# Gate and value products by Strassen's method in a fused attention and two-MLP kernel

## Chip, cores and metric

One NeuronCore of a Trainium2 chip runs the whole program. The metric is the device time of one execution in microseconds (us); the kernel before takes 590.2 us, the median of 3 runs (589.99 to 590.84).

## What is computed

```python
attn = softmax(mask(q @ k.T / 8)) @ v          # 2 batches, 12 heads, 448 tokens, 64 wide
x = rows of 768 (12 heads x 64) for 896 tokens
h = x @ w_in;  y = (h * clip(h + 3, 0, 6) / 6) @ w_out             # 768 -> 2048 -> 768
xn = y / sqrt(mean(y * y) + 1e-6) * rms_g
out = (silu(xn @ w_gate) * (xn @ w_val)) @ w_out2                  # 768 -> 1536 -> 768
```

The weights come as float64 and are narrowed to float32 on the chip.

## The kernel before

Activations lie transposed: features on the partitions, tokens along the row. The 896 tokens are two groups g of 448 columns, so that one PSUM bank (128 x 448 float32) is one output tile of a group. Each float32 operand is split into a high half (a cast to fp32r) and a low half (the rest), and a product of two tiles is three matmuls (`mm3`, lines 199 to 208): high by high, high weights by low, low weights by high.

The work runs in this order: attention for both groups with the first MLP's first layer of group 0 laid between its steps; `ff1_in(1)` (16 tiles of 18 matmuls); `ff1_out(0)` and `ff1_out(1)` (6 tiles of 48 matmuls each); `ff2_in` (lines 592 to 603: 12 weight columns m, gate and value, both groups, 48 tiles of 18 matmuls); and `strassen` (lines 498 to 522: the last product by Strassen's method in its Winograd form, 7 products of 54 matmuls).

The order on every engine's queue is written by hand. The program counts steps (lines 83 to 97 and 700 to 711); in a step after attention nine matmuls are issued, and `at(delay, fn)` puts other work at the head of a later step, in the order in which it was asked for. An engine takes its instructions strictly in that order. A tile of 18 matmuls is two steps.

Weights pass through `w_load` (line 116, a DMA), `w_split` and `narrowed` (lines 135 to 159: two passes over the 64-bit words, on ScalarE, or one of them on GpSimd where `beside` is set), `w_join` (line 165, VectorE), `w_halves` (line 176, ScalarE cast) and `w_low` (line 183, VectorE subtraction). Three weight tiles are split ahead of their use; there are four buffers for halves (NW), three for raw words (NRAW), three for narrowed tiles (NC_BUF). `w_tile` (line 191) asks for the next split when a tile is first used. `b_prepare` to `b_keep` (lines 211 to 261) narrow the last weight, form Strassen's sums of it and store them in DRAM; this runs every 6 steps from the middle of `ff1_out(1)` into `ff2_in`.

The RMS norm is applied late. `ff1_y` and `ff1_ylow` (lines 558 to 574) multiply y by rms_g, split it and sum the squares on GpSimd; `rms_sum` (a matmul with ones), `rms_root` and `rms_inv` (lines 576 to 587) make the inverse root, and `ff2_gate` and `ff2_val` (lines 605 to 625) multiply it onto each output tile. The left operands of the last product and their sums (`sums_first` to `sums_third`, lines 455 to 475) stay in SBUF until `a_split` and `a_low` (lines 477 to 494) halve them.

Of the kernel before, what the change touches and what calls it, by code (L numbers as in the profile page):

```python
# [9 lines left out]
F32 = mybir.dt.float32  # L10
# [38 lines left out]
def fused_kernel(ctx: ExitStack, tc, qa, qb, ka, kb, v, w_in, w_out, w_gate, w_val, w_out2, rms_g, out):  # L49
# [36 lines left out]
    def at(delay, fn, *args):  # L86
        due[clock["now"] + delay].append((fn, args))
# [18 lines left out]
    for m in range(NF2):  # L106
        srcs += [w_gate[m], w_val[m]]
    srcs += [(p, n) for p in ORDER for n in range(NN)]
    IN2 = 4 * NP1
    OUT2 = IN2 + 2 * NF2  # L110
    raws, plain, splits = {}, {}, {}

    apart = {n: APART for n in range(NW - 1)}
    state = {"load": 0, "split": 0}

    def w_load():
        n = state["load"]
        if n >= len(srcs):
# [12 lines left out]
        c = wpool.tile([128, 768], F32, tag="c", name=f"c{n}", bufs=NC_BUF)  # L131
        nc.sync.dma_start(c, src)
        plain[n] = c

    def w_split():

        n = state["split"]
        if n >= len(srcs):
# [51 lines left out]

    def w_tile(n, j):

        if n not in used:
# [16 lines left out]

    def b_prepare(column, part):

        raw = wpool.tile([128, 768, 2], U32, tag="braw", name=f"braw{column}_{part}", bufs=1)
# [235 lines left out]
        for k in range(NF1):  # L449
            gs.pop((g, k))  # L450

    left, halves = {"split": set()}, {}
    SOURCE = {1: (0, 0), 2: (0, 1), 4: (1, 1), 7: (1, 0)}

    def sums_first(p):

        t = slot([128, NT], f"s1_{p}")
        nc.vector.tensor_add(t, left[1, 2 * p], left[1, 2 * p + 1])
        left["s1", p] = t
        nc.vector.tensor_sub(left[1, 2 * p], left[0, 2 * p], left[1, 2 * p])  # L460
        at(1, sums_second, p)

    def sums_second(p):
        if (1, p) not in left["split"]:
            at(1, sums_second, p)
            return
        a = left[0, 2 * p]
        nc.vector.tensor_sub(a, left["s1", p], a)
        left["s2", p] = a
        at(1, sums_third, p)  # L470

    def sums_third(p):
        t = slot([128, NT], f"s4_{p}")
        nc.vector.tensor_sub(t, left[0, 2 * p + 1], left["s2", p])
        left["s4", p] = t

    def a_split(q, p):

        key = {5: ("s1", p), 6: ("s2", p), 3: ("s4", p)}.get(q)
        if key is None:  # L480
            g, odd = SOURCE[q]
            key = (g, 2 * p + odd)
        src = left[key]
# [4 lines left out]
        at(1, a_low, q, p, key, hi, lo, src)  # L488

    def a_low(q, p, key, hi, lo, src):  # L490
        nc.vector.tensor_sub(lo, src, f32(hi))
        left["split"].add((q, p))
        if q != 1:
            left.pop(key)

    bank, held = {}, {}

    def strassen(w0):

        kps = NF2 // 2  # L500
        seen = set()
        for i, q in enumerate(ORDER):
            if i + 1 < len(ORDER):
                for p in range(kps):
                    at(1 + p, a_split, ORDER[i + 1], p)
            for n in range(NN):
# [49 lines left out]
                ff2_store(0, 2 * n, ps)  # L556

    def ff1_y(g, m, ps):
        hi = slot([128, NT], f"yhi{g}_{m}", F32R)
        nc.scalar.mul(hi, ps, gvec[:, m:m + 1])  # L560
        s = slot([128, NT], f"sq{g}_{m}")
        nc.scalar.activation(s, ps, AF.Square)
        at(1, ff1_ylow, g, m, ps, hi, s)

    def ff1_ylow(g, m, ps, hi, s):
        lo = slot([128, NT], f"ylo{g}_{m}", F32R)
        nc.vector.scalar_tensor_tensor(lo, ps, gvec[:, m:m + 1], f32(hi), ALU.mult, ALU.subtract)
        ys[g, m] = (hi, lo)
        if m == 0:
            ri[g] = s  # L570
            return
        nc.gpsimd.tensor_add(ri[g], ri[g], s)
        if m == NK - 1:
            at(2, rms_sum, g)

    def rms_sum(g):
        ps = psum(f"n{g}")[:, :NT]
# [14 lines left out]
    def ff2_in(w0):
        for m in range(NF2):
            for n in range(2):
                for g in range(2):
                    ps = psum(f"f{g}_{m}_{n}")[:, :NT]
                    ks = range(NK)
                    for k in ks:
                        yield from mm3(ps, w_tile(w0 + 2 * m + n, k), ys[g, k], k == ks[0], k == ks[-1])
                    if n == 0:  # L600
                        at(1, ff2_gate, g, m, ps)
                    else:
                        at(2, ff2_val, g, m, ps)

    def ff2_gate(g, m, ps):
        if g not in inverse:
            at(1, ff2_gate, g, m, ps)
            return
        t = slot([128, NT], f"t{g}_{m}")
        nc.vector.tensor_mul(t, ps, ri[g])  # L610
        ss[g, m] = t
        at(1, ff2_silu, t)

    def ff2_silu(t):
        nc.scalar.activation(t, t, AF.Silu)

    def ff2_val(g, m, ps):
        t = slot([128, NT], f"u{g}_{m}")
        nc.vector.tensor_mul(t, ps, ri[g])
        nc.vector.tensor_mul(t, t, ss.pop((g, m)))  # L620
        left[g, m] = t
        if g == 0 and m % 2 == 0:
            at(1, a_split, 1, m // 2)
        if g == 1 and m % 2 == 1:
            at(2, sums_first, m // 2)

    def ff2_store(g, m, o):
        dst = out[m * 128:(m + 1) * 128, g * NT:(g + 1) * NT]
# [9 lines left out]
        nc.sync.dma_start(dst[:, a], o[:, a])  # L638
        nc.scalar.dma_start(dst[:, b], o[:, b])

    def products():
        yield from ff1_in(0, 0)
        yield from ff1_in(1, NP1)
        yield from ff1_out(0, 2 * NP1)
        for i in range(2 * NK):
            n, rest = divmod(i, 4)
            at(PREP + BETWEEN * i, b_prepare, 2 * n + rest % 2, rest // 2)
        yield from ff1_out(1, 3 * NP1)
        yield from ff2_in(IN2)
        yield from strassen(OUT2)  # L650

    with tc.manual_schedule():
# [115 lines left out]
```

## Time and profile before

| | us |
|---|---|
| median of the runs | 590.2 |
| the profiled execution | 589.9 |
| its span, first to last instruction | 588.1 |
| TensorE (PE) busy in the span | 578.7 |
| VectorE (DVE) busy | 375.2 |
| ScalarE (ACT) busy | 356.5 |
| GpSimd (POOL) busy | 87.2 |

The mean granted TensorE clock is 0.997 of full speed. A busy time is the sum of an engine's instruction times in the span; matmuls are pipelined, so that one lasts about twice the distance to the next, and the pace is read from their starts. A row of a group gives line, engine, operation, output and inputs, shape, count, busy time in us, mean ns of one, and then the engine's idle time before it with what ended it.

### The profile page before, as it was taken

The page shows a single profiled execution, that of the slowest core. Times are in us where ns is not written, and L with a number is a line of the kernel's source. Part 1 is how long each engine was busy: PE and PEld are TensorE (multiplying, and loading weights), DVE is VectorE, ACT ScalarE, POOL GpSimd, SP SyncE. Part 2 cuts the span into 40 slices and gives each one's busy share as a digit, 9 for nine tenths or more (in the row PEclk, how much of TensorE's full clock was granted, in tenths as well). Part 3 has the DMA queues.
Part 4 walks back from the last instruction along what each step waited for, and adds up shares of the span by engine and source line. Part 5 has one row for each costly group of instructions (what it writes and reads, how often), then busy time and mean ns, then how long its engine had stood idle before and what let it go on. Part 6 is the DMA issues. An engine that isn't in the chain of part 4 may idle for free.

```text
span 588.1 us, 8933 instructions
## 1 busy us (share of the span) xinstructions
PE 578.7 (98%) x3138; PEld 507.6 (86%) x3138; DVE 375.2 (64%) x712; ACT 356.5 (61%) x682; POOL 87.2 (15%) x132
## 2 busy tenths in 40 slices
PE   8899999999999999999999999999999999999997
PEld 6557777778899999999999999999999999999996
DVE  4767777676455576664466677978665655675861
ACT  7998888887455587774355885565444432354440
POOL 5665444544000000101010100000000000000000
PEclk9999999999999999999999999999999999999999
DMA  8968776762233469975668966875623202133531
GB/s 229 283 191 253 228 248 205 236 196 86 68 111 116 190 242 319 330 251 169 238 209 321 341 204 229 301 249 175 204 91 126 81 28 81 54 111 106 171 116 64
DMA packets 41149, 109.52 MB, mean 186 GB/s; under 512 B 5648, under 2 KB 20176, under 8 KB 41104
## 3 DMA queue, kind: packets, MB, share of 16 engines
q1 hardware_dynamic: 40672, 108.60, 55.7%
q8 instruction: 25, 0.41, 0.3%
q10 hardware_dynamic: 432, 0.34, 0.2%
q14 instruction: 20, 0.16, 0.1%
HBM read 85.33 MB, written 23.59 MB: 185 GB/s over the span
## 4 chain that ended last, share of the span: by engine, by line
PE 93%; ACT 6%; issue 1%; DVE 0%; DVEq 0%
PE f L203 10%; PE f L207 10%; PE f L205 10%; PE y L203 8%; PE y L207 8%; PE y L205 8%; PE h L207 7%; PE h L203 7%; PE h L205 7%; ACT sm L330 4%; PE o L390 3%; PE t L364 3%; PE s L313 3%; PE z L203 1%; PE z L207 1%; PE z L205 1%
## 5 line engine op out<-in xcount | busy, mean ns | idle before, releaser
L179 ACT CAST whi<-c 128x768 fp32r<-128x768 f32 x109 | 90.9, 834 | 94.0 <-DVE c L163 50.5
L185 DVE TENSOR_TENSOR wlo<-c,whi 128x768 fp32r<-128x768 f32 x109 | 108.3, 994 | 27.5 <-ACT whi L179 24.0
L203 PE MATMUL f<-yhi,whi 128*128 128x448 f32 x288 | 105.8, 367 | 0.0
L207 PE MATMUL f<-yhi,wlo 128*128 128x448 f32 x288 | 104.9, 364 | 0.0
L205 PE MATMUL f<-ylo,whi 128*128 128x448 f32 x288 | 104.0, 361 | 0.0
L207 PE MATMUL h<-xh,wlo 128*128 128x448 f32 x192 | 72.0, 375 | 0.0
L205 PE MATMUL h<-xl,whi 128*128 128x448 f32 x192 | 70.9, 369 | 0.0
L203 PE MATMUL y<-ghi,whi 128*128 128x448 f32 x192 | 70.5, 367 | 0.0
L203 PE MATMUL h<-xh,whi 128*128 128x448 f32 x192 | 70.4, 367 | 0.0
L207 PE MATMUL y<-ghi,wlo 128*128 128x448 f32 x192 | 70.0, 365 | 0.0
L205 PE MATMUL y<-glo,whi 128*128 128x448 f32 x192 | 69.3, 361 | 0.0
L163 DVE SCALAR_TENSOR_TENSOR c<-c,raw 128x768 uint32<-128x768 uint32 x56 | 55.7, 995 | 19.0 <-ACT raw L158 12.7
L348 POOL TENSOR_SCALAR sm<-sm,st 112x112 f32<-112x112 f32 (+1 forms) x96 | 55.9, 601 | 68.2 <-ACT pt L374 28.8
L207 PEld LDWEIGHTS f<-yhi,wlo 128*128 128x128 f32 x288 | 53.9, 187 | 5.4 <-issue 0.2
L205 PEld LDWEIGHTS f<-ylo,whi 128*128 128x128 f32 x288 | 54.1, 188 | 4.0
L203 PEld LDWEIGHTS f<-yhi,whi 128*128 128x128 f32 x288 | 54.1, 188 | 3.7 <-issue 0.2
L154 ACT ACTIVATE c<-raw 128x768 f32<-128x768 f32 x56 | 50.8, 907 | 3.4 <-DVE wlo L185 3.4
L330 ACT ACTIVATE sm<-sm,st 112x112 f32<-112x112 f32 (+3 forms) x96 | 49.6, 525 | 3.5 <-DVE st L323 3.4
L427 DVE SCALAR_TENSOR_TENSOR t<-t,h 128x448 f32<-128x448 f32 x32 | 19.8, 620 | 38.7 <-ACT t L423 38.7
L207 PEld LDWEIGHTS h<-xh,wlo 128*128 128x128 f32 x192 | 36.0, 188 | 9.3 <-issue 6.7
L423 ACT ACTIVATE t<-h,half 128x448 f32<-128x448 f32 x32 | 20.4, 638 | 35.4 <-PE h L207 35.4
L323 DVE CUSTOM_DVE_ANT_0 sm<-s,mask 112x112 f32<-112x112 f32 (+3 forms) x96 | 37.3, 443 | 5.9 <-PE s L313 5.6
(106 smaller groups left out, 954.6 us busy)
## 6 DMA issues: line engine op xcount, KB each, us to landing
raw<-in_w_in SPq DMA_DIRECT2D x16, 768.0 KB, 5.7
raw<-in_w_out SPq DMA_DIRECT2D x16, 768.0 KB, 6.0
braw<-in_w_out SPq DMA_DIRECT2D x12, 768.0 KB, 5.7
raw<-in_w_gate SPq DMA_DIRECT2D x12, 768.0 KB, 5.4
raw<-in_w_val SPq DMA_DIRECT2D x12, 768.0 KB, 5.1
c<-kept SPq DMA_DIRECT2D x21, 384.0 KB, 3.0
keptin<-c SPq DMA_DIRECT2D x16, 384.0 KB, 2.7
c<-keptin SPq DMA_DIRECT2D x16, 384.0 KB, 3.0
```

What stands on the lines that cost most here:

```text
L154: nc.scalar.activation(c, f32(high), AF.Prelu, scale=2.0 ** -112, alpha=2.0 ** 32)
L163: nc.vector.scalar_tensor_tensor(bits, bits, 3, z, ALU.logical_shift_left, ALU.bitwise_or)
L179: nc.scalar.copy(hi, c)
L185: nc.vector.tensor_sub(lo, c, f32(hi))
L203: nc.tensor.matmul(ps, whi, xhi, start=first, stop=False, skip_group_check=again)
L205: nc.tensor.matmul(ps, whi, xlo, start=False, stop=False, skip_group_check=again)
L207: nc.tensor.matmul(ps, wlo, xhi, start=False, stop=last, skip_group_check=again)
L323: nc.vector.tensor_tensor_reduce(dst, src, mask[:, S - n:], scale=-0.125, scalar=3e38, op0=ALU.add, op1=ALU.min, accum_out=st[u][:, 0, c:c ...
L330: nc.scalar.activation(dst, dst, AF.Exp, scale=-1.0, bias=st[u][:, 0, c:c + 1], accum_out=st[u][:, 1, c:c + 1])
L348: nc.gpsimd.tensor_scalar(t[:, o:o + n], t[:, o:o + n], c, 1.0, op0=ALU.mult, op1=ALU.mult)
L423: nc.scalar.activation(t, ps, AF.Relu, bias=half, scale=1.0 / 6.0)
L427: nc.vector.scalar_tensor_tensor(t, t, 1.0, ps, ALU.min, ALU.mult)
```

## The change

Nine of the twelve column pairs (gate m, value m) are no longer 4 tiles of 18 matmuls but 7 Strassen products of 9: the halves of the 768 inputs, gate and value, and the two token groups are the 2 x 2 x 2 blocks. Three pairs stay as they were, ahead of the others and in another order (`ff2_plain`). Three of the seven results are added up in PSUM: ScalarE copies a finished bank into another bank (product 1), or to SBUF before more is added onto the same bank (products 7 and 6). y is multiplied by the inverse root before the layer; its halves and the four sums of its blocks are made there. The weight sums of a pair are made on the chip a block ahead (`pair_begin`), with one narrowing pass on GpSimd. Left operands of the last product go to DRAM and come back, except for the last of six. `b_prepare` is moved ahead: six parts into `ff1_in(1)`, six into `ff1_out(1)`, using the buffers of the raw words. The diff is cut; lines of "..." stand for what is left out: the bodies of the `pair_*` helpers, each one subtraction of 128 x 384 (DVE) or one cast (ACT) and its low half (DVE), and changes of names.

```diff
-PREP, BETWEEN = 4, 6
+PREPS = (2, 4, 6), (1, 3.7, 6)
+PLAIN = 3
...
+    def left_keep(q, p, t):
+        if p == NF2 // 2 - 1:
+            fetched[q, p] = t
+            return
+        d = dram.tile([128, NT], F32, name=f"left{q}_{p}")
+        nc.sync.dma_start(d, t)
+        stored[q, p] = d
...
+    def sums_second(p):
+        a = left.pop((0, 2 * p))
+        nc.vector.tensor_sub(a, left.pop(("s1", p)), a)
+        left_keep(6, p, a)
+        t = slot([128, NT], f"s4_{p}")
+        nc.vector.tensor_sub(t, left.pop((0, 2 * p + 1)), a)
+        left_keep(3, p, t)
...
@@ in strassen(w0) @@
                 for p in range(kps):
                     at(1 + p, a_split, ORDER[i + 1], p)
+                    if p >= 3:
+                        at(p - 2, a_fetch, ORDER[i + 1], p)
+            if i + 2 < len(ORDER):
+                for p in range(3):
+                    at(4 + p, a_fetch, ORDER[i + 2], p)
...
@@ in ff1_y(g, m, ps) @@
+        y = slot([128, NT], f"y{g}_{m}")
+        nc.scalar.mul(y, ps, gvec[:, m:m + 1])
         s = slot([128, NT], f"sq{g}_{m}")
         nc.scalar.activation(s, ps, AF.Square)
+        ys[g, m] = y
...
+        elif m < NK - 1:
+            at(1, rms_add, g, s)
+        else:
+            nc.vector.tensor_add(ri[g], ri[g], s)
+            at(1, rms_sum, g)
...
@@ in rms_root(g, ps) @@
         nc.vector.reciprocal(ri[g], ri[g])
+        for i, k in enumerate((0, 1, 2, 3, 4, 5)):
+            at(1 + (i // 2 if g else 2 * i), y_scale, g, k)
+        if g:
+            for j in range(KH):
+                at(6 + j, y_sums, j)
+    def y_scale(g, k):
+        y = ys[g, k]
+        nc.vector.tensor_mul(y, y, ri[g])
+        at(1, y_split, {(0, 0): 1, (0, 1): 2, (1, 0): 0, (1, 1): 4}[g, k // KH], k % KH, y)
+    def y_split(q, j, src):
...
+        nc.scalar.copy(hi, src)
+        at(1, y_low, q, j, hi, lo, src)
...
+        nc.vector.tensor_sub(lo, src, f32(hi))
+    def y_sums(j):
+        a21, a22 = ys[1, j], ys[1, j + KH]
+        nc.vector.tensor_add(a22, a21, a22)
+        nc.vector.tensor_sub(a21, ys[0, j], a21)
+        at(1, y_split, 5, j, ys[1, j + KH])
+        at(1, y_split, 7, j, ys.pop((1, j)))
+        at(1, y_more, j)
+    def y_more(j):
+        a11, a12 = ys.pop((0, j)), ys.pop((0, j + KH))
+        nc.vector.tensor_sub(a11, ys.pop((1, j + KH)), a11)
+        nc.vector.tensor_sub(a12, a12, a11)
+        at(1, y_split, 6, j, a11)
+        at(2, y_split, 3, j, a12)
+    def ff2_plain(w0):
+        order = [(g, i) for g in range(2) for i in range(4)]
+        order += [(g, i) for i in range(4, 2 * PLAIN) for g in range(2)]
+        for t, (g, i) in enumerate(order):
+            m, n = divmod(i, 2)
...
+            if t == 0:
+                at(1, w_split)
+            elif t in (5, 6) or t >= 8 and t % 2 == 0:
+                splits.pop(w0 + (t - 5 if t < 8 else i - 1), None)
+                at(1, w_split)
...
+    def pair_begin(m):
+        at(1, pair_narrow, m, 0)
+        at(2, pair_narrow, m, 1)
+        at(3, pair_high, m, 0)
+        at(4, pair_first, m)
+        at(5, pair_second, m)
+        at(6, pair_third, m)
+        at(7, pair_high, m, 1)
+        at(8, pair_low, m, 1)
+        if m + 1 < NF2:
+            at(4, pair_load, m + 1, 0)
+            at(5, pair_load, m + 1, 1)
...
+    def ff2_strassen():
+        order = []
+        for m in range(PLAIN, NF2):
+            order.append((1, m))
+            if m > PLAIN:
+                order.append((3, m - 1))
+            order += [(q, m) for q in (7, 6, 2, 5, 4)]
+        order.append((3, NF2 - 1))
...
+            name = {1: "x", 2: "x", 7: "r", 4: "r"}.get(q, "y")
...
+            for j in range(KH):
+                yield from mm3(ps, pair_tile(q, m, j), ops[q, j], q in (1, 7) and j == 0, j == KH - 1,
+                               q not in (1, 7))
...
+            at(1, ff2_combine, q, m)
+    def ff2_combine(q, m):
+        if q == 1:
+            y = spare.pop(0)
+            fb["y", m] = y
+            nc.scalar.copy(y, fb["x", m])
+        elif q == 7:
...
+            nc.scalar.copy(fh["c22", m], fb["r", m])
+        elif q == 6:
...
+            nc.scalar.copy(fh["c21", m], fb["y", m])
+        elif q == 2:
...
+            nc.scalar.activation(fh["s", m], fb.pop(("x", m)), AF.Silu)
+        elif q == 5:
+            t = fh["c22", m]
+            nc.vector.tensor_add(t, fb["y", m], t)
+        elif q == 4:
+            t = fh["c21", m]
+            nc.vector.tensor_add(t, fb.pop(("r", m)), t)
+            at(1, ff2_silu, t)
+            at(2, ff2_out, m)
+        else:
...
+            nc.vector.tensor_mul(t, y, t)
+            spare.append(y)
+            left_ready(0, m, t)
```

## Rows read from the trace of the kernel before

**Rows 1.** The page, busy time (share of the span) and instructions of engines.
```profile
PE 578.7 (98%) x3138; PEld 507.6 (86%) x3138; DVE 375.2 (64%) x712; ACT 356.5 (61%) x682; POOL 87.2 (15%) x132
```
**Rows 2.** The page, chain that ended last: share of the span by engine.
```profile
PE 93%; ACT 6%; issue 1%; DVE 0%; DVEq 0%
```
**Rows 3.** Busy time by stage: `ff1_in(1)`, `ff2_in`, `strassen` (the header names the columns).
```profile
core 0: us, PE busy (x) PEld busy (x) DVE busy (x) ACT busy (x) POOL busy (x), PEclk, DMA share, GB/s
158.00:215.30 57.30, 57.30 (x285) 53.12 (x284) 34.58 (x49) 33.39 (x52) 0.00 (x0) 1.00 0.42 146
...
332.50:508.10 175.60, 175.60 (x869) 162.46 (x868) 116.18 (x174) 88.30 (x119) 1.17 (x1) 1.00 0.48 162
508.10:588.10 80.00, 76.59 (x379) 70.66 (x377) 49.82 (x78) 32.58 (x56) 0.00 (x0) 1.00 0.34 109
```
**Rows 4.** Tiles f and w: duration ns min/median/max, first and last start us.
```profile
L203 PE MATMUL f<-yhi,whi x288: 367/367/368, 332.6 to 507.5; 128*128 128x448 f32 x144
...
L203 PE MATMUL w<-ahi,whi x12: 367/367/368, 508.1 to 514.8; 128*128 128x448 f32 x12
```
**Rows 5.** Timeline of PE around the matmul with ones: start, duration.
```profile
280.50 0.36 PE L205 MATMUL y<-glo,whi 128*128 128x448 f32 x1
280.70 0.91 PE L578 MATMUL n<-sq,ones 128*128 128x448 f32 x2
...
281.65 0.37 PE L203 MATMUL y<-ghi,whi 128*128 128x448 f32 x1
```
**Rows 6.** Groups of DVE instructions, shapes apart.
```profile
L185 DVE TENSOR_TENSOR wlo<-c,whi 128x768 fp32r<-128x768 f32 x109 | 108.3, 994 | 27.5 <-ACT whi L179 24.0 <-PE y L207 1.0
...
L229 DVE SCALAR_TENSOR_TENSOR b<-braw 128x384 uint32<-128x384 uint32 x24 | 12.3, 554 | 6.6 <-ACT braw L158 6.6
...
L474 DVE TENSOR_TENSOR s<-u,u 128x448 f32<-128x448 f32 x6 | 3.7, 616 | 0.0
```
**Rows 7.** Timeline of DVE in `ff2_in`: start, duration.
```profile
342.76 2.95 DVE L586 RECIPROCAL sq<-sq 128x448 f32<-128x448 f32 x1 [0.92 <-ACT sq L582]
345.85 0.62 DVE L610 TENSOR_TENSOR t<-f,sq 128x448 f32<-128x448 f32 x1
...
352.04 0.62 DVE L620 TENSOR_TENSOR u<-u,t 128x448 f32<-128x448 f32 x1
352.58 0.62 DVE L491 TENSOR_TENSOR alo<-u,ahi 128x448 fp32r<-128x448 f32 x1
353.12 0.95 DVE L163 SCALAR_TENSOR_TENSOR c<-c,raw 128x768 uint32<-128x768 uint32 x1
353.99 0.62 DVE L610 TENSOR_TENSOR t<-f,sq 128x448 f32<-128x448 f32 x1
354.52 1.02 DVE L229 SCALAR_TENSOR_TENSOR b<-braw 128x384 uint32<-128x384 uint32 x2
355.45 0.95 DVE L185 TENSOR_TENSOR wlo<-c,whi 128x768 fp32r<-128x768 f32 x1
```
**Rows 8.** Groups of ACT instructions, shapes apart.
```profile
L179 ACT CAST whi<-c 128x768 fp32r<-128x768 f32 x109 | 90.9, 834 | 94.0 <-DVE c L163 50.5 <-PE y L205 22.8 <-PE z L205 9.3
...
L154 ACT ACTIVATE c<-raw 128x768 f32<-128x768 f32 x56 | 50.8, 907 | 3.4 <-DVE wlo L185 3.4
...
L486 ACT CAST ahi<-u 128x448 fp32r<-128x448 f32 x30 | 15.8, 564 | 8.3 <-DVE u L620 8.3
...
L528 ACT COPY e<-w 128x448 f32<-128x448 f32 x2 | 1.1, 534 | 3.9 <-PE w L207 3.9
```
**Rows 9.** Timelines of POOL and DVE where a narrowing on POOL meets a join.
```profile
68.79 0.92 POOL L156 TENSOR_SCALAR raw<-raw 128x768 uint32<-128x768 uint8 x1
...
68.99 1.53 DVE L163 SCALAR_TENSOR_TENSOR c<-c,raw 128x768 uint32<-128x768 uint32 x1 [0.23 <-ACT c L154]
```
**Rows 10.** DMA issues: KB each, median us from issue to landing.
```profile
raw<-in_w_gate SPq DMA_DIRECT2D x12, 768.0 KB, 5.4
...
c<-kept SPq DMA_DIRECT2D x21, 384.0 KB, 3.0
```

More of the change, by code (lines that the diff above doesn't have):

```diff
@@ L105, in fused_kernel @@
         srcs += [a[n] for n in range(NP1)] + [(name, n) for n in range(NP1)]
-    for m in range(NF2):
+    for m in range(PLAIN):
         srcs += [w_gate[m], w_val[m]]
+    IN2 = 4 * NP1
+    OUT2 = IN2 + 2 * PLAIN
     srcs += [(p, n) for p in ORDER for n in range(NN)]
-    IN2 = 4 * NP1
-    OUT2 = IN2 + 2 * NF2
     raws, plain, splits = {}, {}, {}
     apart = {n: APART for n in range(NW - 1)}
-    state = {"load": 0, "split": 0}
+    state = {"load": 0, "split": 0, "limit": OUT2}
     def w_load():
         n = state["load"]
-        if n >= len(srcs):
+        if n >= state["limit"]:
             return
@@ L191, in w_tile @@
     def w_tile(n, j):
-        if n not in used:
+        if n not in used and not IN2 <= n < OUT2:
             used.add(n)
@@ L211, in b_prepare @@
     def b_prepare(column, part):
-        raw = wpool.tile([128, 768, 2], U32, tag="braw", name=f"braw{column}_{part}", bufs=1)
+        raw = wpool.tile([128, 768, 2], U32, tag="raw", name=f"braw{column}_{part}", bufs=NRAW)
         nc.sync.dma_start(raw.rearrange("p n t -> p (n t)"), w_out2[2 * column + part].bitcast(U32))
@@ L450, in ff1_out, with left_ready, a_fetch @@
             gs.pop((g, k))
-    left, halves = {"split": set()}, {}
-    SOURCE = {1: (0, 0), 2: (0, 1), 4: (1, 1), 7: (1, 0)}
+    left, stored, fetched, halves = {}, {}, {}, {}
+    def left_keep(q, p, t):
[5 more added lines that the diff above has]
+        stored[q, p] = d
+    def left_ready(g, m, t):
+        left[g, m] = t
+        p, odd = divmod(m, 2)
+        q = {(0, 0): 1, (0, 1): 2, (1, 1): 4}.get((g, odd))
+        if q:
+            left_keep(q, p, t)
+        if all((i, 2 * p + j) in left for i in range(2) for j in range(2)):
+            at(1, sums_first, p)
     def sums_first(p):
         t = slot([128, NT], f"s1_{p}")
-        nc.vector.tensor_add(t, left[1, 2 * p], left[1, 2 * p + 1])
+        nc.vector.tensor_add(t, left[1, 2 * p], left.pop((1, 2 * p + 1)))
         left["s1", p] = t
-        nc.vector.tensor_sub(left[1, 2 * p], left[0, 2 * p], left[1, 2 * p])
+        left_keep(5, p, t)
+        d = left.pop((1, 2 * p))
+        nc.vector.tensor_sub(d, left[0, 2 * p], d)
+        left_keep(7, p, d)
         at(1, sums_second, p)
     def sums_second(p):
-        if (1, p) not in left["split"]:
-            at(1, sums_second, p)
-            return
[L467 to L475, printed above, removed]
-    def a_split(q, p):
[L479 to L483, printed above, removed]
+        a = left.pop((0, 2 * p))
[4 more added lines that the diff above has]
+        left_keep(3, p, t)
+    def a_fetch(q, p):
+        if p == NF2 // 2 - 1:
+            return
+        t = slot([128, NT], f"a{q}_{p}")
+        nc.sync.dma_start(t, stored.pop((q, p)))
+        fetched[q, p] = t
+    def a_split(q, p):
+        src = fetched.pop((q, p))
         hi = slot([128, NT], f"ahi{q}_{p}", F32R)
@@ new lines, in fused_kernel, with y_low @@
+    done = set()
+    def y_low(q, j, hi, lo, src):
+        nc.vector.tensor_sub(lo, src, f32(hi))
+        done.add((q, j))
+    def y_sums(j):
+        assert (0, j) in done and (4, j) in done
+        a21, a22 = ys[1, j], ys[1, j + KH]
[10 more added lines that the diff above has]
+        at(2, y_split, 3, j, a12)
@@ new lines, in fused_kernel @@
+    ss, spare = {}, []
+    def ff2_plain(w0):
[3 more added lines that the diff above has]
+            m, n = divmod(i, 2)
+            if t < 2:
+                splits.pop(w0 + t - 2, None)
+            if t == 0:
[3 more added lines that the diff above has]
+                at(1, w_split)
+            elif t == 7:
+                splits.pop(w0 + 2)
+            if t == len(order) - 6:
+                at(1, pair_load, PLAIN, 0)
+                at(2, pair_load, PLAIN, 1)
+            if t == len(order) - 4:
+                pair_begin(PLAIN)
+            ps = psum(f"f{g}_{i}")[:, :NT]
+            for k in range(NK):
+                q = ((1, 2), (0, 4))[g][k // KH]
+                yield from mm3(ps, w_tile(w0 + i, k), ops[q, k % KH], k == 0, k == NK - 1)
+            if n == 0:
+                at(1, ff2_gate, g, m, ps)
+            else:
+                at(2, ff2_val, g, m, ps)
+                if m == PLAIN - 1:
+                    spare.append(ps)
+        splits.pop(w0 + 2 * PLAIN - 1)
+        for j in range(KH):
+            ops.pop((0, j))
@@ L605, in ff2_gate, with ff2_val, pair_load @@
     def ff2_gate(g, m, ps):
-        if g not in inverse:
-            at(1, ff2_gate, g, m, ps)
-            return
         t = slot([128, NT], f"t{g}_{m}")
-        nc.vector.tensor_mul(t, ps, ri[g])
+        nc.scalar.activation(t, ps, AF.Silu)
         ss[g, m] = t
-        at(1, ff2_silu, t)
+    def ff2_val(g, m, ps):
+        t = ss.pop((g, m))
+        nc.vector.tensor_mul(t, ps, t)
+        left_ready(g, m, t)
+    praw, pc, ph = {}, {}, {}
+    HALF = slice(0, 384), slice(384, 768)
+    def pair_load(m, i):
+        t = wpool.tile([128, 768, 2], U32, tag="raw", name=f"praw{m}_{i}", bufs=NRAW)
+        nc.sync.dma_start(t.rearrange("p n t -> p (n t)"), (w_gate, w_val)[i][m].bitcast(U32))
+        praw[m, i] = t
@@ new lines, in pair_begin, with pair_narrow @@
+    def pair_begin(m):
[10 more added lines that the diff above has]
+            at(5, pair_load, m + 1, 1)
+    def pair_narrow(m, i):
+        raw = praw.pop((m, i))
+        c = wpool.tile([128, 768], F32, tag="c", name=f"pc{m}_{i}", bufs=NC_BUF)
+        z = narrowed(c, raw, True)
+        pc[i] = c
+        at(1, joined, c, z)
@@ new lines, in pair_high, with pair_low, pair_t, pair_t_high @@
+    def pair_high(m, i):
+        hi = wpool.tile([128, 768], F32R, tag="whi", name=f"phi{m}_{i}", bufs=NW)
+        lo = wpool.tile([128, 768], F32R, tag="wlo", name=f"plo{m}_{i}", bufs=NW)
+        nc.scalar.copy(hi, pc[i])
+        ph[m, i] = (hi, lo)
+    def pair_low(m, i):
+        hi, lo = ph[m, i]
+        nc.vector.tensor_sub(lo, pc.pop(i), f32(hi))
+    def pair_t(m, q, a, b):
+        t = slot([128, 384], f"pt{m}_{q}")
+        nc.vector.tensor_sub(t, a, b)
+        pc["t", q] = t
+    def pair_t_high(m, q):
+        hi = slot([128, 384], f"pthi{m}_{q}", F32R)
+        lo = slot([128, 384], f"ptlo{m}_{q}", F32R)
+        nc.scalar.copy(hi, pc["t", q])
+        ph[m, "t", q] = (hi, lo)
@@ new lines, in pair_t_low, with pair_first, pair_second @@
+    def pair_t_low(m, q):
+        hi, lo = ph[m, "t", q]
+        nc.vector.tensor_sub(lo, pc.pop(("t", q)), f32(hi))
+    def pair_first(m):
+        gate, val = pc[0], pc[1]
+        pair_t(m, 7, val[:, HALF[1]], val[:, HALF[0]])
+        pair_t(m, 5, val[:, HALF[0]], gate[:, HALF[0]])
+        pair_low(m, 0)
+        pc["b21"] = gate
+    def pair_second(m):
+        val, gate = pc[1], pc.pop("b21")
+        pair_t(m, 6, val[:, HALF[1]], pc["t", 5])
+        nc.vector.tensor_sub(val[:, HALF[0]], gate[:, HALF[1]], pc["t", 6])
+        pair_t_high(m, 7)
+        pair_t_high(m, 5)
@@ new lines, in pair_third, with pair_tile @@
+    def pair_third(m):
+        pair_t_low(m, 7)
+        pair_t_high(m, 6)
+        at(1, pair_t_low, m, 5)
+        at(1, pair_t_low, m, 6)
+    def pair_tile(q, m, j):
+        if q in (5, 6, 7):
+            key, o = (m, "t", q), 0
+        else:
+            key, o = {1: ((m, 0), 0), 2: ((m, 0), 384), 4: ((m, 1), 0), 3: ((m, 1), 384)}[q]
+        w = tuple(t[:, o + j * 128:o + j * 128 + 128] for t in ph[key])
+        if j == KH - 1 and q not in (1, 4):
+            ph.pop(key)
+        return w
@@ new lines, in fused_kernel @@
+    fb, fh = {}, {}
+    def ff2_strassen():
[6 more added lines that the diff above has]
+        order.append((3, NF2 - 1))
+        for q, m in order:
+            if q == 1 and m + 1 < NF2:
+                pair_begin(m + 1)
+            if q == 1 and m + 1 == NF2:
+                state["limit"] = len(srcs)
+                for n in range(NRAW):
+                    at(1 + n, w_load)
+                for n in range(NW - 1):
+                    at(4 + n, w_split)
+                for p in range(NF2 // 2):
+                    at(1 + p // 2, a_fetch, ORDER[0], p)
+                    at(4 + p // 2, a_split, ORDER[0], p)
+                for p in range(3):
+                    at(5 + p, a_fetch, ORDER[1], p)
+            name = {1: "x", 2: "x", 7: "r", 4: "r"}.get(q, "y")
+            if q in (1, 7):
+                fb[name, m] = psum(f"f{name}_{m}")[:, :NT]
+            ps = fb[name, m]
+            for j in range(KH):
+                yield from mm3(ps, pair_tile(q, m, j), ops[q, j], q in (1, 7) and j == 0, j == KH - 1,
+                               q not in (1, 7))
+                if m == NF2 - 1:
+                    ops.pop((q, j))
+            at(1, ff2_combine, q, m)
+        spare.clear()
@@ L614, in ff2_silu, with ff2_out @@
     def ff2_silu(t):
         nc.scalar.activation(t, t, AF.Silu)
[L617 to L625, printed above, removed]
+    def ff2_out(m):
+        t = fh.pop(("c22", m))
+        nc.vector.tensor_mul(t, t, fh.pop(("c21", m)))
+        left_ready(1, m, t)
@@ L639, in ff2_store, with plan_preps @@
         nc.scalar.dma_start(dst[:, b], o[:, b])
+    def plan_preps(i0, first, between, count):
+        for i in range(count):
+            n, rest = divmod(i0 + i, 4)
+            at(first + int(between * i), b_prepare, 2 * n + rest % 2, rest // 2)
     def products():
         yield from ff1_in(0, 0)
+        plan_preps(0, *PREPS[0])
         yield from ff1_in(1, NP1)
         yield from ff1_out(0, 2 * NP1)
-        for i in range(2 * NK):
-            n, rest = divmod(i, 4)
-            at(PREP + BETWEEN * i, b_prepare, 2 * n + rest % 2, rest // 2)
+        plan_preps(PREPS[0][2], *PREPS[1])
         yield from ff1_out(1, 3 * NP1)
-        yield from ff2_in(IN2)
+        yield from ff2_plain(IN2)
+        yield from ff2_strassen()
         yield from strassen(OUT2)
```

47 lines of the change are left out of this document (15 added, 32 removed).

## The prediction

> **What bounds the kernel now.** I read the page first: PE is busy 98% of the span, DVE 64% [rows 1], and the chain that ended last lies on PE for 93% of it [rows 2]. Then the windows by stage: in the gate/value layer PE is busy for all of its 175.6 us at a granted clock of 1.00 (the 2.4 GHz level), with DVE busy for 116.2 and ACT for 88.3 of it [rows 3]. The tile rows give the pace: the layer's first matmul starts at 332.6, the first of the next product at 508.1 [rows 4]; between them lie 864 matmuls and one matmul with ones, which pushes its neighbours 0.75 apart (280.50 to 281.65 for what would take two paces of 0.2) [rows 5]. So a matmul costs (175.5 - 0.75) / 864 = 0.202 us, and nothing else costs PE anything in this stage. A matmul removed is worth 0.202 as long as the other engines keep up; that is the whole question.
>
> **What is removed.** 9 column pairs x 4 tiles x 18 = 648 matmuls become 9 x 7 x 9 = 567: 81 fewer, 81 x 0.202 = **-16.4 us**. The other three pairs (216) and the last product keep their counts. No other PE work is added.
>
> A step is nine matmuls, 1.82 us, and in the new part it is exactly one Strassen product. I went through the queues step by step, with the distance between starts of queued DVE instructions as their price: 128 x 448 0.54 (352.58 to 353.12), 128 x 768 0.87 (353.12 to 353.99), 128 x 384 0.47 (two from 354.52 to 355.45), and 3.09 from the reciprocal's start to that of the next [rows 7]. Their own durations, 0.616, 0.994 and 0.554 [rows 6], are the upper ends.
>
> **The norm ahead of the layer.** Let 0 be the layer's first matmul. ACT scales and squares the last y tile (0.56 and 0.53 by its nearest rows [rows 8]) and DVE adds, done at about 2.0. The matmul with ones stands 18 matmuls in, at 3.6, so PE does not wait; it ends at 4.6 [rows 5], the root at 5.2, the reciprocal lets the next go at 8.3. Group 0 was made ready a stage earlier, and four of its tiles (14.6 us) come first. Group 1 needs its first low half at 14.6 + 0.75 + 0.2 = 15.6; DVE has by then done six scalings, one weight subtraction, one value product and one low half, 8 x 0.54 + 0.87 on top of 8.3 = 13.5. No wait there, with 2 us to spare.
>
> The next need is tighter. The ninth tile starts at 8 x 18 x 0.202 + 0.75 = 29.9 and wants the low half of the fifth weight tile at its third matmul, 30.3. That subtraction is queued on DVE behind nearly everything that the new input needs: 6 scalings, 6 low halves, 12 block sums, 11 of the 12 low halves of those sums, and 3 value products, 38 of 128 x 448 (20.5), and with it 3 instructions of 128 x 768 (2.6). DVE gets there without a gap from 8.3 on: 8.3 + 20.5 + 2.6 = 31.4, end 31.5. PE waits **1.2 us**. The first narrowing on POOL falls into this stretch as well (its raw words are loaded early); it may block a DVE instruction for up to 0.9 (below), I take 0.5. The sum is **+1.7**. Ends: 0, if DVE's order leaves it no later than PE; by the full durations 38 x 0.616 + 3 x 0.994 + 8.3 = 34.7, so 4.4, and 0.9 for POOL, 5.3. I take the distances, as these are queued instructions. After it DVE is through with the sums and meets PE again: to the Strassen part's first low half it has some 7 us of work for 12 us.
>
> **One Strassen block** is 63 matmuls, 12.7 us. DVE: two joins and two low halves of 128 x 768, seven instructions of 128 x 384, four combinations and on average two sums of 128 x 448: 4 x 0.87 + 7 x 0.47 + 6 x 0.54 = 10.0, or 11.6 by durations. ACT: two narrowing passes 1.8, two casts 1.7, three casts of 128 x 384 at under 0.56 each, three bank copies 1.6 and two Silu of about 0.6: 8.0 [rows 8]. Both fit. The seeds: bank y is copied by ACT (0.534 [rows 8]) between the end of product 6 and the start of product 5, one product or 1.82 us later; 1.2 is left for hand-over and for what is queued ahead on ACT, two casts which wait for a DVE subtraction of a step before, due some 2 us earlier. The other two copies have two products' time (in the first block one). PE's reads of weight halves come at least two steps after their making. I take **0**; the upper end is worked out as a rival.
>
> POOL narrows two tiles in each block. Where it did so beside a join, DVE's instruction, begun 0.20 into POOL's 0.92, took 1.53 [rows 9] against 0.994 for its form's like [rows 6]. So I count up to 2 x 0.92 of blocked DVE per block: 11.9 by distances, still under 12.7; 13.4 by durations.
>
> The Trainium skill (SBUF — State Buffer, Who interferes with whom) states that a VectorE instruction with two SBUF inputs and a GpSimd instruction that reads SBUF exclude each other, the later one waiting until the first ends; by that all 18 narrowings either wait or block, and the sum would go from 575.5 towards 581.4 if DVE always were the one to wait and took its durations. The pair of rows just named agrees with it: 0.54 longer of 0.72 overlapped.
>
> **What is moved or added beside PE.** `b_prepare`'s twelve parts each issue one load of 768 KB, two ACT passes of about 0.9, two joins and two or so subtractions (four DVE instructions of 0.55), and three to four stores. Six now fall into `ff1_in(1)`, where DVE is busy 34.6 and ACT 33.4 of 57.3 us [rows 3]: 34.6 + 6 x 2.2 = 48 and 33.4 + 6 x 1.8 = 44. What PE waits for there, weight halves, is made three tiles (11 us) ahead; cost 0. They leave `ff2_in`, which is what frees DVE there. On SP's queue they stand before the raw loads of the next stage, whose buffers they share; each part holds one of three buffers for four steps, and raw loads land in 5.4 us [rows 10] with three steps to do so; 0, at most one late load, 3 us. The stores and loads of left operands (35 of 224 KB each way) stand on SP behind DVE's sums, and pair loads behind them: a pair load has four steps (7.3 us) for 5.4. Loads back are asked for three steps (5.5 us) before their cast; a larger one landed in 3.0 [rows 10]; 0, at most 1 us. The last product's casts and combinations are as before, with DVE busy 49.8 of 80.0 [rows 3], so the tail is unchanged.
>
> **Sum.** The profiled execution took 589.9, its span 588.1: 589.9 - 16.4 + 1.7 = 575.2. The median of the runs is 0.3 higher: **575.5**.
>
> **Rivals.** (1) No wait: DVE reaches the fifth weight tile in time. For it: 1.2 us is 4% of a chain that I added up from single rows. Against: it has no slack in it. 573.8. Chance 0.20. (2) DVE becomes the bound in the Strassen blocks, by POOL blocking it: 13.4 against 12.7, 0.65 x 9 = 5.9 more, 581.4. For it: rows 9, and 90% busy by durations. Against: distances, not durations, governed the queued stretch [rows 7], and POOL can wait as well. Its band is 578 to 586. Chance 0.14. This is the mechanism that the rule of the Trainium skill named above would give. (3) Slower: the seeds. PE waits for ACT's copy in each block, since ACT takes its casts first and these wait for DVE. It decides once the copy comes more than 1.2 + 16.4 / 9 = 3.0 us late in every block; with ACT two steps behind it is 9 x (3.64 - 1.2) = 22 us of waiting, 575.5 + 22 = 597. Against: ACT has 4.7 us free in each block. Chance 0.06; a milder form that just eats the gain, within 0.2% (1.2 us, about what a measurement of this kernel can tell from no change), 0.03. (4) Several small waits of these kinds together, 586 to 589: 0.07.
>
> **How the numbers follow.** The forecast, 574.2 to 577.9 by its own ends, has 0.50. The range 573.4 to 582.0 takes in the forecast, rival 1 and most of rival 2 (0.10), 0.80 in all. Below 573.8, less the runs' own spread, there is nothing: PE's remaining matmuls would run without gaps. Faster by over 0.2%: 0.50 + 0.20 + 0.14 + 0.07 = 0.91; same 0.03; slower 0.06.
>
> **What would show it.** Right: 81 fewer matmuls at the same 0.202; one gap on PE of 1 to 3 us some 30 us into the layer, ended by the DVE low half of a weight tile; DVE busy without idle before it; blocks of 12.7 us after it, PE full. Wrong: PE gaps in each block ended by an ACT copy of a bank (rival 3) or by a DVE low half of a pair's weights (rival 2), gaps in the first tiles of group 1, or in the last product ended by a load.

## The result and the profile after

The change takes 581.62 us, the median of 4 runs (578.33 to 583.29), against 590.34 before; the ratio is 0.9845, 95% interval 0.9801 to 0.9889. That is 8.7 us faster, where 14.8 was forecast: inside the range, above the forecast's own band. The runs also spread over 5 us, where those before spread over 0.85 (in a later series of 17 runs of the kernel before, two took 592.5 and 595.3, so a wide spread isn't the change's alone).

The profiled execution took 582.0, its span 580.2. Busy times on the page, which answer to [rows 1]:

```profile
PE 566.5 (98%) x3057; PEld 493.6 (85%) x3057; DVE 409.5 (71%) x783; ACT 376.0 (65%) x740; POOL 105.1 (18%) x148
```

PE has 81 instructions fewer, exactly as counted. Then the stages, as in [rows 3]: a stretch behind the ninth tile, the nine Strassen blocks, the last product.

```profile
core 0: us, PE busy (x) PEld busy (x) DVE busy (x) ACT busy (x) POOL busy (x), PEclk, DMA share, GB/s
369.50:372.00 2.50, 2.50 (x7) 2.25 (x8) 2.08 (x3) 1.70 (x3) 2.04 (x1) 0.50 0.00 0
385.20:500.20 115.00, 115.00 (x569) 106.35 (x569) 94.02 (x148) 64.25 (x111) 14.78 (x15) 1.00 0.54 184
500.20:580.20 80.00, 76.58 (x379) 70.66 (x377) 49.90 (x78) 33.37 (x58) 0.00 (x0) 1.00 0.56 190
```

The blocks take 115.0 us for 567 matmuls, 0.203 each, and PE is busy throughout: the Strassen part as such costs nothing but its matmuls. The last product takes the 80.0 of before, with its left operands coming from DRAM. What is missing from the gain lies ahead of the blocks. The tile rows that answer to [rows 4] give the layer's first matmul and the end of the layer:

```profile
L204 PE MATMUL f<-yhi,whi x72: 361/361/575, 334.8 to 384.6; 128*128 128x448 f32 x72
...
L204 PE MATMUL w<-ahi,whi x12: 361/361/361, 500.2 to 506.9; 128*128 128x448 f32 x12
```

The layer starts at 334.8, 2.2 later than before, and some matmuls in it last 575 ns. The timeline of PE shows two gaps (start, duration; in brackets the wait and what ended it):

```profile
338.07 0.36 PE L206 MATMUL f<-ylo,whi 128*128 128x448 f32 x1
340.29 1.02 PE L596 MATMUL n<-sq,ones 128*128 128x448 f32 x2 [1.86 <-DVE sq L588]
...
367.03 0.37 PE L206 MATMUL f<-ylo,whi 128*128 128x448 f32 x1
369.40 0.65 PE L208 MATMUL f<-yhi,wlo 128*128 128x448 f32 x1 [2.00 <-DVE wlo L186]
369.85 0.57 PE L204 MATMUL f<-yhi,whi 128*128 128x448 f32 x1
...
372.83 0.42 PE L208 MATMUL f<-yhi,wlo 128*128 128x448 f32 x1
373.09 0.36 PE L204 MATMUL f<-yhi,whi 128*128 128x448 f32 x1
```

First comes a wait of 1.86 ahead of the matmul with ones, which I had put at nothing. Then the ninth tile waits at its third matmul for the low half of the fifth weight tile, as forecast; the distance is 2.37 in place of 0.20, so 2.2 lost. Behind it ten matmuls take 3.69 us (369.40 to 373.09) in place of 2.02: the clock was granted at 0.50, the 1.2 GHz level, in the window above. Put together: 589.9 - 16.4 + 2.2 (late start) + 1.9 (ahead of the ones) + 2.2 (ninth tile) + 1.7 (clock) = 581.5, of 582.0.

On DVE the stretch before the ninth tile looks as the sum had it (some of its instructions):

```profile
342.02 2.95 DVE L601 RECIPROCAL sq<-sq 128x448 f32<-128x448 f32 x1
345.00 1.16 DVE L613 TENSOR_TENSOR y<-y,sq 128x448 f32<-128x448 f32 x2
...
353.49 0.62 DVE L634 TENSOR_TENSOR y<-y,y 128x448 f32<-128x448 f32 x1
354.03 0.62 DVE L633 TENSOR_TENSOR y<-y,y 128x448 f32<-128x448 f32 x1
354.68 0.62 DVE L634 TENSOR_TENSOR y<-y,y 128x448 f32<-128x448 f32 x1
...
361.06 1.19 DVE L642 TENSOR_TENSOR y<-y,y 128x448 f32<-128x448 f32 x1
...
368.39 0.95 DVE L186 TENSOR_TENSOR wlo<-c,whi 128x768 fp32r<-128x768 f32 x1
```

No row has a bracket, so DVE never stands idle from 342.0 to 369.3. A block sum that uses the result of the one before, or overwrites one of its inputs, starts 0.65 behind it, not 0.54 (354.03 to 354.68), and one block sum took 1.19 while POOL ran its first narrowing.

### The profile page after: what moved, and what is told of

Its sections match the earlier page's. It is cut to its first block, busy times and chain, and to the rows that moved or that the text cites. A ratio compares the mean times of both kernels' runs of the same rounds, so it can differ in the third digit from the quotient of the medians.

```text
span 580.2 us, 9124 instructions
## 1 busy us (share of the span) xinstructions
PE 566.5 (98%) x3057; PEld 493.6 (85%) x3057; DVE 409.5 (71%) x783; ACT 376.0 (65%) x740; POOL 105.1 (18%) x148
## 4 chain that ended last, share of the span: by engine, by line
PE 82%; DVE 6%; DMA 4%; ACT 4%; SPq 3%; issue 2%; DVEq 0%
PE h L208 7%; PE h L204 7%; PE h L206 7%; PE y L208 6%; PE y L204 6%; PE y L206 6%; PE f L208 4%; PE f L204 4%; PE f L206 4%; PE o L391 3%; PE t L365 3%; PE s L314 3%; PE fr L208 2%; PE fx L204 2%; PE fx L208 2%; PE fr L206 2%
## 5 line engine op out<-in xcount | busy, mean ns | idle before, releaser
L186 DVE TENSOR_TENSOR wlo<-c,whi 128x768 fp32r<-128x768 f32 x91 | 90.4, 996 | 24.2 <-ACT whi L180 21.7
L180 ACT CAST whi<-c 128x768 fp32r<-128x768 f32 x91 | 76.1, 837 | 46.9 <-DVE c L164 25.9
L164 DVE SCALAR_TENSOR_TENSOR c<-c,raw 128x768 uint32<-128x768 uint32 x38 | 38.5, 1014 | 18.6 <-ACT raw L159 12.4
L157 POOL TENSOR_SCALAR praw<-praw 128x768 uint32<-128x768 uint8 x18 | 19.3, 1074 | 122.7 <-DMA praw<-in_w_gate 74.9
L208 PEld LDWEIGHTS y<-ghi,wlo 128*128 128x128 f32 x192 | 35.9, 187 | 5.0 <-DVE wlo L186 1.6
L204 PEld LDWEIGHTS y<-ghi,whi 128*128 128x128 f32 x192 | 36.0, 188 | 3.5 <-ACT whi L180 1.0
L206 PEld LDWEIGHTS h<-xl,whi 128*128 128x128 f32 x192 | 36.0, 188 | 2.8
L206 PEld LDWEIGHTS y<-glo,whi 128*128 128x128 f32 x192 | 36.0, 188 | 2.8
L204 PEld LDWEIGHTS h<-xh,whi 128*128 128x128 f32 x192 | 36.2, 188 | 2.5
L428 DVE SCALAR_TENSOR_TENSOR t<-t,h 128x448 f32<-128x448 f32 x32 | 19.8, 618 | 24.5 <-ACT t L424 24.5
L365 PE MATMUL t<-ident,sm 112*112 112x112 f32 x240 | 33.1, 269 | 2.9 <-POOL sm L349 2.4
```

The lines of the kernel that those rows point to most:

```text
L157: nc.gpsimd.tensor_scalar(low, byte, 1.0 / 32.0, -15.5 / 32.0, op0=ALU.mult, op1=ALU.add)
L164: nc.vector.scalar_tensor_tensor(bits, bits, 3, z, ALU.logical_shift_left, ALU.bitwise_or)
L180: nc.scalar.copy(hi, c)
L186: nc.vector.tensor_sub(lo, c, f32(hi))
L204: nc.tensor.matmul(ps, whi, xhi, start=first, stop=False, skip_group_check=again)
L206: nc.tensor.matmul(ps, whi, xlo, start=False, stop=False, skip_group_check=again)
```

## The experiments

| run | median us (range) | ratio to before, 95% interval |
|---|---|---|
| e0_after, the change again | 580.73 (578.32 to 582.22) | 0.9832 (0.9811 to 0.9854) |
| e1_lead | 577.61 (576.38 to 577.90) | 0.9779 (0.9766 to 0.9793) |
| e2_late | 586.36 (584.46 to 586.46) | 0.9919 (0.9905 to 0.9934) |
| e4_both | 580.20 (579.23 to 580.58) | 0.9826 (0.9813 to 0.9840) |
| e7_all | 577.78 (576.78 to 578.69) | 0.9776 (0.9749 to 0.9802) |
| e3_fill | 576.38 (576.10 to 576.71) | 0.9751 (0.9726 to 0.9776) |
| e5_undo | 591.75 (590.30 to 595.09) | 1.0015 (0.9995 to 1.0035) |
| e6_nopool | 580.62 (579.64 to 581.07) | 0.9821 (0.9789 to 0.9852) |
| e9_first | 575.74 (574.96 to 576.19) | 0.9750 (0.9737 to 0.9763) |

**The change again**, with no edit:

> The changed kernel as it is, beside the next three on one chip. By its own four runs 578 to 583 us, against 590.3 before. What is to be seen again: the layer's first matmul some 2 us later than before (334.8 against 332.6), a wait of about 1.9 us ahead of the matmul with ones, a wait of about 2.2 us at the ninth tile, and some 3.4 us at half the clock behind it.

Its profile, of the fastest run (578.3), has the wait ahead of the ones (1.70) and that of the ninth tile (2.02), but the layer starts at 333.1 and the clock stays at its upper level behind the same wait. So the late start and the slow stretch differ between these two executions; the two waits stay.

**Earlier raw loads.**

```diff
-        at(3, b_narrow, column, part, raw)
+        at(lead, b_narrow, column, part, raw)
...
-            at(first + int(between * i), b_prepare, 2 * n + rest % 2, rest // 2)
+            early = min(2, first + int(between * i) - 1) if i0 else 0
+            at(first + int(between * i) - early, b_prepare, 2 * n + rest % 2, rest // 2, 3 + early)
```

> The six parts of the moved weight preparation in the second MLP product of group 1 load their raw words two steps earlier (five ahead of their narrowing in place of three), all else as in the changed kernel. Theory A (loads too close to their use: ACT, in order, waits for raw words that land in 7.1 us when asked for 5.5 ahead, and with it the casts of the weights that PE needs, and the norm): the layer starts at 332.6 to 333.0, the wait ahead of the matmul with ones falls under 0.5, the time falls by about 4, to 577.5. Theory B (the transfers themselves are the limit in that stage, so asking earlier only makes them queue longer): the layer still starts at 334 or later and the time stays at 581.6.

Theory A held. ACT's waits for these raw words between 274 and 335, the changed kernel first and then this run (waiter, awaited, us in total, times, longest):

```profile
ACT braw L155 <- DMA braw<-in_w_out: 19.8, 5, 8.1
```

```profile
ACT braw L155 <- DMA braw<-in_w_out: 1.4, 2, 0.9
```

The wait ahead of the ones is gone. The layer starts at 333.1, as it did in the profile of e0_after without the edit; so the late start is better read from the two products ahead of the layer, by the first and the last start of one of their matmuls (before, changed kernel, this run):

```profile
L203 PE MATMUL y<-ghi,whi x192: 367/367/368, 215.4 to 332.0; 128*128 128x448 f32 x192
```

```profile
L204 PE MATMUL y<-ghi,whi x192: 361/367/468, 215.5 to 334.2; 128*128 128x448 f32 x192
```

```profile
L204 PE MATMUL y<-ghi,whi x192: 367/367/368, 215.8 to 332.5; 128*128 128x448 f32 x192
```

That is 116.6, 118.7 and 116.7 us. The other traces agree: 117.2, 119.5 and 118.1 with the short lead in this place (e0_after, e2_late, e6_nopool), 116.6 in all four others with the longer one (e3_fill, e4_both, e7_all, e9_first). The load itself lands in 6.5 us against 7.1, and from 300 to 333 the stage moves 305 GB/s, where the changed kernel moved 290: the transfers were not the limit, the distance between asking and use was. ACT takes its instructions in order; five times it stood before raw words of a weight that PE doesn't use before 500, with the casts and the norm that PE needed next queued behind. The median falls by 3.1 against the run beside it.

**Later block sums**, alone and with the earlier loads:

```diff
-                at(6 + j, y_sums, j)
+                at(10 + j, y_sums, j)
```

> The block sums of the new input are asked for four steps later, so that the fifth plain weight tile's low half comes ahead of most of them on DVE. Theory A (DVE's order made the wait at the ninth tile, and the wait made the clock fall): no wait there (under 0.3), granted clock 1.00 throughout, 2.2 + 1.7 = 3.9 less, 577.7. Rival (the work is only put off, and DVE is short of time in the whole plain part): a wait of 2 us or more comes at the first Strassen products instead, and the time stays at 581.6.

> Earlier loads and later sums together. If the two losses are separate, both go: 581.6 - 4.1 - 3.9 = 573.6, which is the matmuls alone. If one hides the other (an earlier start of the norm already gives DVE the time at the ninth tile, or the loads cannot come earlier), about 577.5.

Theory A has the ninth tile right, which no longer waits, but not the time: the first Strassen block waits instead, as the rival has it (PE's waits, the run with the later sums alone):

```profile
PE f L204 <- ACT f L818: 2.4, 2, 2.2
...
PE fr L208 <- DVE ptlo L745: 1.3, 1, 1.3
PE fx L208 <- DVE plo L730: 0.8, 1, 0.8
```

A wait of 2.0 became three of 4.3 in all: the low halves of the first pair's weights, and a seed, whose copy waits for DVE to finish with that bank. (This profile also has a layer that starts at 336.4 and eight matmuls at the slow pace behind the last of these waits.) The rival's reason, that DVE is short of time in the whole plain part, isn't shown, and its time was too low (586.36 for 581.6). DVE's own timeline has a hole where the sums used to stand:

```profile
359.63 0.96 DVE L164 SCALAR_TENSOR_TENSOR c<-c,raw 128x768 uint32<-128x768 uint32 x1 [4.80 <-ACT raw L159]
```

With the sums put off, the join of a weight tile is next in DVE's queue; its narrowing on ACT stands behind a Silu that waits 5.9 for a tile of PE. So DVE stands idle for 4.8, and the first low half of the first pair's weights starts 36.7 behind the first scaling (346.39 to 383.12), where the changed kernel takes 31.8 (345.00 to 376.80). The changed kernel has no such hole, and at its first block DVE is ahead again: at 385.42 it waits 1.93 for PE. The same hole, of 4.8, is in the traces of e4_both, e7_all and e9_first, which all keep this edit. With the earlier loads the same three waits stay, and the time, 580.20, is 2.6 worse than with the loads alone.

**Less work in that stretch.** Besides both edits, the left sums of pair 0 come later:

```diff
-            at(1, sums_first, p)
+            at(1 if p else 12, sums_first, p)
```

> Earlier loads, block sums four steps later, and the four sums of the first left operands (2.2 us of DVE, needed only in the last product) put off by eleven steps. Theory A (DVE's total work up to the first Strassen block is short of time by some 2 us, so a wait only moves unless work leaves this stretch): the waits at the first Strassen block (0.8, 1.3 and 2.2 us in the run with both edits) go or fall under 1 us in all, clock 1.00, about 574.5. Rival (the seed's copy is late in the first block because of ACT's own order, not of DVE): its wait of about 2 us stays, 576.5.

577.78, above both numbers and no better than the earlier loads alone (577.61). The waits at the low halves are gone, as theory A has it, but the seed's stays, as the rival has it:

```profile
383.96 0.47 PE L204 MATMUL f<-yhi,pthi 128*128 128x448 f32 x1 [1.96 <-ACT f L818]
```

Its own trace names the queue: the seed's copy on ACT starts at 383.39, when DVE has done the value product of the last plain pair, which stands behind a weight subtraction of 1.66 that is needed five products later.

**That order mended**, with the left sums later still (30 steps for 12):

```diff
-                at(2, ff2_val, g, m, ps)
+                at(1 if m == PLAIN - 1 else 2, ff2_val, g, m, ps)
...
-            at(1, ff2_combine, q, m)
+            if (q, m) == (1, PLAIN):
+                ff2_combine(q, m)
+            else:
+                at(1, ff2_combine, q, m)
```

> As the run with all three edits, and the value products of the last plain pair one step earlier on DVE (ahead of a weight subtraction not needed for five products), the first block's seed one step earlier on ACT (ahead of a narrowing pass), and the first left sums put off by 29 steps. Theory A (the first seed was late through its place in the two queues): its wait of 2.0 us goes, and with it the two of 0.2 to 0.4 in the next blocks; PE waits for nothing from the layer's start on, 574.5. Rival (DVE is short of time whatever the order): a wait of 1 to 2 us comes at the low halves of the first blocks, 576 to 577.5.

575.74, 5.0 us less than the change again and 14.5 less than the kernel before beside it (590.25). One wait is left in the layer, at the same seed:

```profile
382.25 0.47 PE L204 MATMUL f<-yhi,pthi 128*128 128x448 f32 x1 [0.38 <-ACT f L821]
```

Theory A held for the seed, though not to the end: 1.2 us over its 574.5 are left. In the trace there are this 0.4, two distances of 0.4 and 0.3 in later blocks, and a layer that starts at 333.5, a delay that is there before the two products ahead of it begin (216.3 for 215.4). The run has both a new order and later left sums; what each gave isn't separated, and the hole of 4.8 on DVE is still in it.

**The gap filled.** With the earlier loads, ten matmuls that nobody reads (an extra to what is computed) stand ahead of the ninth tile's waiting one:

```diff
+                if t == 8 and k == 0:
+                    scratch = psum("fill")[:, :NT]
+                    for _ in range(10):
+                        nc.tensor.matmul(scratch, ops[1, 0][0][:, :128], ops[1, 0][0], start=True, stop=True)
                 yield from mm3(
```

> Earlier loads, and ten more matmuls into a bank that nobody reads, laid ahead of the ninth tile's waiting matmul (2.0 us of work in a wait of 2.0). Theory A (the clock falls since PE stands still there): the granted clock stays 1.00, no run pays the 1.7 us of the slow stretch; against the run with earlier loads alone, which has 576.4 to 577.9, all runs lie at the lower end, 576.0 to 576.5. Rival (the clock falls for another reason): the slow stretch stays in some runs and the spread is as before; or the added matmuls come late and cost up to 2.0, 579.5.

More matmuls, less time: 576.38, all six runs within 0.6 us, against 577.61 with the earlier loads alone. The profile of that run (577.90) has the slow stretch, a little behind the same wait:

```profile
365.50 0.47 PE L208 MATMUL f<-yhi,wlo 128*128 128x448 f32 x1 [2.00 <-DVE wlo L186]
...
367.05 0.58 PE L204 MATMUL f<-yhi,whi 128*128 128x448 f32 x1
```

With the filler the tile waits only 0.2 behind the extra ones (365.20 to 365.59 for a pace of 0.2), and the clock behind it stays at 1.00:

```profile
362.97 2.19 PE L675 MATMUL fill<-yhi 128*128 128x448 f32 x10
365.00 0.36 PE L204 MATMUL f<-yhi,whi 128*128 128x448 f32 x1
365.20 0.37 PE L206 MATMUL f<-ylo,whi 128*128 128x448 f32 x1
365.59 0.47 PE L208 MATMUL f<-yhi,wlo 128*128 128x448 f32 x1
```

```profile
365.00:368.00 3.00, 2.98 (x15) 2.44 (x14) 2.57 (x4) 1.51 (x3) 2.31 (x1) 1.00 0.00 0
```

So it is the standing still that lets the clock fall, in some executions and not in others. The other traces bear it out. From 60 us to the end the granted clock falls to 0.50 five times in all of them, and each time PE stands or has just stood: 2.00 (the change), 2.00 (e1_lead), 2.17 (e2_late), 4.82 and 3.07 (e5_undo, below). It stays at 1.00 behind 2.02 (e0_after), 2.21 (e4_both) and 1.96 (e7_all). The Trainium skill (TensorE: Matmul & The Clock Gate, Part 1: The HAM clock gate) says that inactivity takes the clock to the lower of two levels, which agrees with 0.50 and 1.00.

**The preparation moved back.**

```diff
-        raw = wpool.tile([128, 768, 2], U32, tag="raw", name=f"braw{column}_{part}", bufs=NRAW)
+        raw = wpool.tile([128, 768, 2], U32, tag="braw", name=f"braw{column}_{part}", bufs=1)
...
-        plan_preps(0, *PREPS[0])
...
-        plan_preps(PREPS[0][2], *PREPS[1])
+        plan_preps(0, 4, 6, 2 * NK)
```

> The preparation of the last weight put back to its old place and pace (every six steps from group 1's second product into the layer, with its own buffer), all else as changed. Theory A (the move made the late start): the layer starts at 332.6 to 332.8 and the wait ahead of the matmul with ones goes, 4.1 less; but three parts or so (2.1 us of DVE each) now stand ahead of the ninth tile's weight, whose wait grows from 2.2 to about 8: 581.6 - 4.1 + 6.3 = 584. Rival (the late start comes from the new norm, not from the move): the start stays near 335 and the time is 588.

Neither theory's number: 591.75, no faster than before. Theory A fell: the wait ahead of the matmul with ones didn't go, it grew. The ninth tile's wait grew to 3.1, less than I had, but PE waits in more places (its timeline, from the slowest of its ten runs, 595.09):

```profile
341.83 1.12 PE L596 MATMUL n<-sq,ones 128*128 128x448 f32 x1 [4.82 <-DVE sq L588]
...
375.11 0.74 PE L208 MATMUL f<-yhi,wlo 128*128 128x448 f32 x1 [3.07 <-DVE wlo L186]
...
397.33 0.47 PE L204 MATMUL f<-yhi,pthi 128*128 128x448 f32 x1 [1.38 <-ACT f L818]
...
415.66 0.47 PE L204 MATMUL f<-yhi,pthi 128*128 128x448 f32 x1 [1.67 <-ACT c L824]
430.49 0.47 PE L204 MATMUL f<-yhi,pthi 128*128 128x448 f32 x1 [1.66 <-ACT c L824]
```

Two passes of a part stand among what ACT has to do ahead of the last y tile, and PE waits 4.8 for the norm; and in the blocks the copies come late, which is the rival of the seeds come true in three of nine blocks. Raw words come late here too: between 274 and 335 ACT waits 18.5 us for them (19.8 in the change, 1.7 before). So the move alone didn't make ACT's wait. Six of these loads were issued in this stretch before the change as well (277.5 to 330.0; the preparation begins at the head of `ff1_out(1)`, not in its middle) and landed in 5.4 at 258 GB/s; in this run they land in 7.0 at 218, in the change in 7.1 at 270. Why they land later isn't shown, and the amount moved doesn't explain it. With the preparation left in the layer nothing of the gain remains, but a run with the old place and a longer lead wasn't made, so the place and the short lead aren't separated here.

**GpSimd's pass to ScalarE.**

```diff
-        z = narrowed(c, raw, True)
+        z = narrowed(c, raw, False)
```

> The narrowing pass that GpSimd takes in each Strassen block goes to ScalarE instead (18 passes of about 0.9 us). Theory A (GpSimd's blocking of VectorE is hidden, since PE waited for nothing in the blocks): DVE's busy time in the blocks falls from 94 by at most 10 us, the time stays within 1 us of 581.6, and less only by what the first narrowing saves at the ninth tile (up to 0.6). Rival (the blocking costs PE time): 2 to 6 us faster; or ScalarE, 1.8 us fuller in each block, brings the copies late: up to 9 x 1 us slower.

The time is that of the change (580.62 beside 580.73). The window of its blocks:

```profile
382.80:497.80 115.00, 115.00 (x568) 106.30 (x568) 90.97 (x148) 75.57 (x127) 0.00 (x0) 1.00 0.56 189
```

PE takes 115.0 us as with POOL; DVE is 3.0 us less busy, ACT 11.3 more. The ninth tile's wait is 1.44 in place of 2.00, about the 0.5 that I had put on POOL there.

## Why the prediction was right, and by how much it was off

**The range** held by luck. Its upper end, 582.0, was set there to take in most of rival 2, which didn't happen; 581.62 lies just under it through losses that were priced at 0 or not at all, and one of the four runs, 583.29, lies above it. The forecast's own band, 574.2 to 577.9, doesn't follow from the ends of its one term either: 0 and 5.3 on 573.8 give 573.8 to 579.1.

**The matmuls**: 81 fewer at 0.202, as forecast; nothing to add.

**The ninth tile**: the mechanism, place and order were right, to the instruction. Forecast 1.2 and 0.5 for POOL, measured 2.2. The twelve block sums include six pairs that stand 0.65 apart, which I had priced at 0.54: 0.7 more.

**The Strassen blocks**: forecast 0, and 115.0 for 114.6 says so. Rival 2 fell: by the runs with and without POOL's passes, blocked DVE costs 3.0 us in the window of the blocks, where POOL is busy for 14.8. The Trainium skill (SBUF — State Buffer, Who interferes with whom) gives the rule for it; the trace agrees that such blocking is there (1.19 for 0.62 beside POOL's pass), and not that it decides. Rival 3, the seeds, did not happen in the change, but its slack is small: in e2_late, e4_both, e7_all and e5_undo copies came late.

**What failed** is the step that priced the moved preparation at 0. I compared busy sums with the stage's length and set the load's 5.4 us against three steps of 5.5, as if 0.1 were slack, with a price from other loads in another stage. Here the loads landed in 7.1, and I had looked for the waiting on SP only, where each transfer has its place, not on ACT, where the narrowing stands in line before the casts. It cost 2.2 at the layer's start and 1.9 ahead of the ones in the profiled run; e1_lead, with two steps more of lead, gives back 3.1 in the median. Why the loads landed later than before the change stays open (e5_undo). That no wait stood ahead of the matmul with ones I had from ACT being free at the layer's start, which this broke.

**What was not in the sum** is the clock: 1.7 us in the profiled run, where it fell behind the ninth tile's wait; in e0_after it didn't. So forecast +1.7, measured 2.2 + 1.9 + 2.2 + 1.7 = 8.0 and 0.5 of small change.

## What to carry to other kernels

When PE's work is cut, the work that stays on the other engines falls due sooner: add up, from the last common wait to the first new use, what one in-order queue has to do, and compare it with PE's time for the same stretch. Before work is put off, look at what stands next in that queue: if its inputs aren't there yet, the engine stands idle and the delay comes back later, as here, where one wait of 2.0 became three of 4.3 behind a hole of 4.8. Work for later that is slipped into a queue must have its data there long before its turn, since everything behind it waits too.

## What the runs showed of the hardware

A wait of 2.0 us on PE was followed by some 3.4 us at half the clock in some executions and not in others, in the same kernel and at the same place (369.40 in the changed kernel's profile, none in e0_after), and not where ten matmuls filled the wait (the profile of e3_fill, whose median is 1.2 below that of e1_lead). Queued DVE instructions of 128 x 448 start 0.54 apart where they are independent and 0.65 where one uses the result of the one before or overwrites its input (354.03 to 354.68), with durations of 0.62 in both cases.
